# Turned blocks of e moved two units at a time, and the residual in four transfers, in a threshold attention and MLP mixer kernel

## The chip, the cores and the metric

The kernel runs as one program on one core of one Trainium2 chip. The metric is the device time of one execution in microseconds (us). Before the change three executions took 1266.56, 1267.58 and 1271.94 us; their median is 1267.58 us. Less is better.

A core has five engines that work side by side, each through an instruction list of its own, in order: TensorE (PE in the profile, with its weight loads as PEld), VectorE (DVE), ScalarE (ACT), GpSimd (POOL) and SyncE (SP). In this kernel SP computes nothing: it issues the DMA transfers, one after the other. "SPq" in the profile is SP's list.

## What is computed

For 8 batches b, 8 heads of 576 tokens and 64 columns, and then a mixer over 576 tokens x 512 columns, all in float32:

```python
scores = q @ k.T / 8
thresh = max(scores) - tau                      # per row
e      = exp(where(scores >= thresh, scores, -1e9) - max)
x      = (e / (sum(e) + 1e-9)) @ v              # heads side by side: 576 x 512
u      = x + (relu(x.T @ w_tok1) @ w_tok2).T    # token mixing, 576 -> 256 -> 576
out    = u + relu(u @ w_ch1) @ w_ch2            # channel mixing, 512 -> 1536 -> 512
```

## The kernel before, in words

**Units, rounds, groups.** A pair is two heads of a batch, so a batch has four pairs. The 2 x 576 score rows of two neighbouring pairs are cut into nine units of 128 rows; each unit has the scores of two heads, 128 x 1152 numbers. Two units with consecutive numbers make a round (`make_round`). Three units make a group (GU = 3), which is the size of one product with v (`values`, L365 and L370). Since nine is odd and groups have three units, the two units of a round lie in one group in six rounds of nine, and in two groups in the other three.

**One round.** PE forms the scores (L825). DVE takes the row maxima (mx, L842), POOL makes the bias (L848), ACT masks (L858) and takes exponentials with row sums (L868), DVE inverts the sums (rr, L276 and L277), and POOL scales e (L285). For batch 0, PE turns e (L300). For the seven later batches DVE turns each unit in 32 x 32 blocks into a tile T (`turn_blocks`, L315), and four transfers issued by SP put the blocks in their places in eT (`move`, L327). When a group's three units have landed, PE multiplies eT with v, and ACT or DVE drains the result into xT (L374).

**The mixer of the batch before** runs between the rounds: token mixing (L454, L472, with x turned by L395 and L401 and moved by L406 and L412), then for one block of 256 tokens channel mixing, `make_groups`: twelve products with w_ch1 (L948), drained through relu by ACT (L953) or DVE (L956), then eight with w_ch2 (L964), drained by DVE (L978) with the residual u added. The residual is turned by two DVE transposes into the tile `us` (L933) and moved to `ut` by eight transfers (L940). The sums are written over `us`, from which two stores go to the output (L988). `us` is one buffer, so the next batch's L933 waits for this batch's stores to land. The rest of the blocks is written aside (L531) and done at the end by `Late`, from about 905 us on; that part's instructions are not touched.

**What sets the order.** A planner, `Scheduler`, runs while the program is built. Each step is an `Op` with an engine, a cost in us, what it depends on and a rank. The planner keeps a clock for each engine, takes the step that can start first (then the one of lower rank), and writes the instructions of each engine in that order. For a DMA step, `dmas=(count, KB, issue)` says how many transfers it issues, how large each is, and what one costs SP; `transfer` lets eight be in flight and moves 214 KB per us. So a cost that is edited moves the order of everything planned after it. On the chip each engine then follows its list, and waits where an input is not there.

**Weights** come in as 31 pieces of 64-bit words through three raw buffers (`load_piece`, L200), and are converted by ACT, DVE and POOL (last at 174.75 us in the trace, POOL L239).

Of the kernel before, what the change touches and what calls it, by code (L numbers as in the profile page):

```python
# [17 lines left out]
P = 128  # L18
# [3 lines left out]
def kernel(  # L22
# [166 lines left out]
    def load_piece(i):  # L189
        if i >= len(pieces):  # L190
            return
        dst, src = pieces[i]
        rows = dst.shape[0]
        n = 1
        for d in dst.shape[1:]:
            n *= d
        if i == len(pieces) - 2:
            raw_at[i % NRAW] = att.tile([P, 2 * WMAX], U32, tag="spare", bufs=1, name="spare_a")
        raw = raw_at[i % NRAW][0:rows, 0 : n * (2 if wide(i) else 1)].bitcast(src.dtype)
        nc.sync.dma_start(out=like(raw, dst), in_=src)  # L200
        if wide(i):
            words = raw.bitcast(U32).rearrange("p (n w) -> p n w", w=2)
            h2 = high[0:rows, WMAX * (i % 2) : WMAX * (i % 2) + n]
            raws[i] = like(words[:, :, 0], dst), like(words[:, :, 1], dst), like(h2, dst)
        else:
            raws[i] = like(raw, dst)
# [103 lines left out]
    def turn_blocks(u):  # L310

        b, p0, t = units[u]
        e = st.pop(u)
        T = Ts[u] = att.tile([P, 4, NK * 32], F32, tag="T", bufs=3, name=f"T_{u}")
        nc.vector.transpose(  # L315
            out=T.rearrange("p a (c x) -> p c a x", c=NK), in_=e.rearrange("p (c a x) -> p c a x", c=NK, a=4)
        )

    def move(u):
        b, p0, t = units[u]  # L320
        key, place = (b, p0, t // GU), t % GU
        if place == 0:
            turned_e[key] = att.tile([P, GU, 4, NK * 32], F32, tag="eT", name=f"eT_{u}")
            eTs[key] = turned_e[key].rearrange("p n i (c x) -> p (n i) c x", c=NK)
        T = Ts.pop(u)
        for i in range(4):
            nc.sync.dma_start(  # L327
                out=turned_e[key][:, place, i, :], in_=T[32 * i : 32 * i + 32]
            )
# [389 lines left out]
    CONV = len(pieces)  # L719
    CR = (1, 1, 2)  # L720
# [26 lines left out]
    def make_conversion():  # L747
        for part in range(2):
            put_ac(0, part)
        for i in range(CONV):  # L750
            put_dv(i, 0)
            for part in range(1, 3):
                put_ac(i + 1, part - 1)
                put_dv(i, part)
            put(("pool", i), sched.op("pool", 1.27, lambda i=i: on_gpsimd(i), (key_op("dv", i, 2), key_op("ac", i, 0)), CR[0]))
            put_load(i + NRAW, (key_op("pool", i),))
# [18 lines left out]
    def make_pair(n):  # L775
# [32 lines left out]
        put(("split", n), sched.op("dve" if n >= NP else "pool", 0.25 if n >= NP else 0.5, lambda: split_middle(n), (key_op("loadv", n), free), 2))  # L808
# [110 lines left out]
    def make_groups(b, halves):  # L919
        uT = xTs[b]  # L920
        reads = []
        for i in range(NOW[b]):
# [3 lines left out]
            def new_us(s=s, i=i):  # L926
                s["us"] = work.tile([P, nt, 4, NCC * 32], F32, tag="us", bufs=1, name=f"us_{b}_{i}")

            def turn_u(s=s, i=i):
                new_us(s)  # L930
                s["ut"] = work.tile([P, nt, 4, NCC * 32], F32, tag="ut", bufs=1, name=f"ut_{b}_{i}")
                for m in range(nt):
                    nc.vector.transpose(  # L933
                        out=s["us"][:, m].rearrange("q a (c d) -> q c a d", c=NCC),
                        in_=uT[:, :, GR * i + P * m : GR * i + P * m + P].rearrange("q c (r a) -> q c a r", a=4),
                    )

            def move_u(k, s=s):
                for m in range(nt):
                    nc.sync.dma_start(  # L940
                        out=s["ut"][:, m, k, :], in_=s["us"][32 * k : 32 * k + 32, m]
                    )
# [30 lines left out]
            def leave(bank, t, c, s=s):  # L973
                if not b and "us" not in s:
                    new_us(s)
                o = s["us"][:, t].rearrange("q a x -> q (a x)")[:, P * c : P * c + P]
# [9 lines left out]
            def store(t, s=s, i=i):  # L986
                t0 = GR * i + P * t
                nc.sync.dma_start(out=out[b, t0 : t0 + P, :], in_=s["us"][:, t].rearrange("q a x -> q (a x)"))  # L988
# [3 lines left out]
            if b:  # L992
                turn = sched.op("dve", 1.2, turn_u, have + state["stores"] + state["adds"] + (converted if b == 1 else []), 5)
                reads.append(turn)
                moved = [sched.op("sp", 1.2, lambda k=k, m=move_u: m(k), (turn,), 1, dmas=(nt, 53, 0.645)) for k in range(4)]
# [17 lines left out]
            for t in range(nt):  # L1013
# [19 lines left out]
                stores.append(sched.op("sp", 0.35, lambda t=t, f=store: f(t), outs, 2, dmas=(1, 150, 0.35)))  # L1033
# [55 lines left out]
    def make_round(it):  # L1089
# [28 lines left out]
        for u in us:  # L1118
# [4 lines left out]
            if not b:  # L1123
# [15 lines left out]
                if t % GU == GU - 1:  # L1139
# [4 lines left out]
            deps += [key_op("T", u - 1), key_op("M", u - 3)]  # L1144
            put(("T", u), sched.op("dve", 1.31, lambda u=u: turn_blocks(u), deps, 4))
            put(
                ("M", u),
                sched.op(
                    "sp",
                    2.4,  # L1150
                    lambda u=u: move(u),
                    (key_op("T", u), key_op("V", G - 2) if t % GU == 0 else None),
                    0,
                    after=(key_op("M", u - 1),),
                    dmas=(4, 147, 0.645),
                ),
            )
            if t % GU == GU - 1:
# [329 lines left out]
```

## Time and profile before

| What | Value |
|---|---|
| three executions, median | 1267.58 us (1266.56 to 1271.94) |
| the profiled execution | 1273.39 us, of which the span from first to last instruction 1271.4 us |
| PE busy in the span | 1237.8 us |
| mean granted TensorE clock | 0.991 |
| eT<-T (L327): transfers, KB each, time to landing | 504, 144 KB, median 3.0 us (2.7 to 5.4) |
| ... SP's time for one issue | 542 / 602 / 2039 ns (least, median, most) |
| ut<-us (L940): transfers issued | 48, SP's median 602 ns, landing median 2.1 us |
| out_dram<-us (L988): transfers, landing | 16, median 3.2 us (2.0 to 4.6) |
| DVE T<-e (L315) | 126 times, median 1369 ns |
| DVE us<-xT (L933) | 12 times from 117 to 860 us, mean 1088 ns |

The page gives busy time per engine, the span in 40 slices, and the chain of work that ended last. A row of the timeline has start, duration, engine, line, operation and tile; what stands in brackets at its end is how long the engine was idle before it and what ended that. A row of the windows view has, for a stretch of time, each engine's busy us with the number of instructions, then the granted clock of TensorE (1.00 is full speed), the mean busy share of the DMA engines and GB/s.

### The profile page before, as it was taken

How to read it: one execution, taken by the hardware profiler on the slowest of the kernel's cores; microseconds unless marked ns; L12 is line 12 of the kernel's file. 1: busy time of each engine (PE TensorE's matmuls, PEld its weight loads, DVE VectorE, ACT ScalarE, POOL GpSimd, SP SyncE). 2: the span in 40 equal slices, each digit the busy share in tenths (PEclk: the TensorE clock that was granted, in tenths of full speed). 3: DMA queues.
4: the chain of work that ended last, by engine and by line, in shares of the span. 5: the costliest groups of instructions: out<-in, count | busy, mean ns of one | idle time of the engine just before them, and what ended most of it. 6: DMA issues, size and time to landing. Idle time of an engine off the chain costs nothing.

```text
span 1271.4 us, 21773 instructions
## 1 busy us (share of the span) xinstructions
PE 1237.8 (97%) x8150; PEld 1015.3 (80%) x8150; DVE 755.0 (59%) x1163; ACT 564.0 (44%) x1233; POOL 315.4 (25%) x518
## 2 busy tenths in 40 slices
PE   8888999999999999999989999999999999999998
PEld 7656778797678778878867777888988888888887
DVE  6699982656666667756666756761443534444443
ACT  6998862554645545556465455531110202011120
POOL 4565641232223333323323322410001010000100
PEclk9899999999999999999999999999999999999999
DMA  9546985366777786786776875750212101021011
GB/s 167 139 124 166 214 212 131 87 128 160 168 164 175 160 169 150 165 178 137 179 148 135 187 159 111 179 150 1 60 23 67 34 25 42 18 67 25 26 34 33
DMA packets 324216, 149.23 MB, mean 117 GB/s; under 512 B 223696, under 2 KB 316880, under 8 KB 324112
## 3 DMA queue, kind: packets, MB, share of 16 engines
q1 hardware_dynamic: 322240, 147.64, 50.5%
q8 instruction: 64, 1.05, 0.4%
q10 hardware_dynamic: 1872, 0.21, 0.1%
q14 instruction: 40, 0.33, 0.1%
HBM read 47.32 MB, written 13.50 MB: 48 GB/s over the span
## 4 chain that ended last, share of the span: by engine, by line
PE 78%; SPq 6%; DVE 5%; DMA 5%; ACT 4%; issue 2%; POOL 0%; DVEq 0%; ACTq 0%; POOLq 0%
PE bank L964 11%; PE bank L948 10%; PE o L1309 10%; PE sc L825 9%; PE bank L370 7%; PE hx L1309 6%; PE bank L454 5%; PE hmm L1309 4%; PE oz L1309 4%; PE hz L1309 4%; PE bank L472 4%; SPq L327 3%; PE bank L365 2%; DVE mx L842 2%; ACT e L858 2%
## 5 line engine op out<-in xcount | busy, mean ns | idle before, releaser
L285 POOL TENSOR_SCALAR e<-e,rr 128x576 f32<-128x576 f32 x288 | 213.2, 758 | 299.1 <-DVE rr L277 286.6
L858 ACT ACTIVATE e<-sc,bias 128x576 f32<-128x576 f32 x288 | 194.1, 740 | 156.8 <-POOL bias L848 155.1
L842 DVE TENSOR_REDUCE mx<-sc 128x2 f32<-128x1152 f32 x144 | 188.1, 1347 | 58.9 <-PE sc L825 58.4
L868 ACT ACTIVATE e<-e,ntau 128x576 f32<-128x576 f32 x288 | 220.4, 778 | 0.3
L315 DVE STREAM_TRANSPOSE T<-e 128x1152 f32<-128x1152 f32 x126 | 170.0, 1362 | 36.1 <-POOL e L285 22.2
L948 PE MATMUL bank<-xT,wc 128*128 128x256 f32 x768 | 181.0, 389 | 6.1 <-ACT g L953 5.1
L964 PEld LDWEIGHTS bank<-wc,g 128*128 128x128 f32 x1536 | 178.0, 192 | 10.4 <-issue 2.4
L964 PE MATMUL bank<-wc,g 128*128 128x128 f32 x1536 | 181.4, 276 | 0.9 <-DVE xT L483 0.4
L948 PEld LDWEIGHTS bank<-xT,wc 128*128 128x128 f32 x768 | 144.2, 192 | 36.6 <-ACT g L953 6.5
L825 PE MATMUL sc<-kT,qT 64*128 64x192 f32 (+1 forms) x1920 | 168.8, 337 | 2.7 <-ACT e L858 2.7
L825 PEld LDWEIGHTS sc<-kT,qT 64*128 64x128 f32 (+1 forms) x1920 | 140.8, 179 | 32.1 <-issue 16.3
L370 PE MATMUL bank<-eT,lv 128*64 128x384 f32 (+1 forms) x1024 | 135.2, 406 | 0.0
L1392 POOL TENSOR_TENSOR us<-us,ut 128x256 f32<-128x256 f32 x27 | 22.4, 843 | 391.8 <-DVE us L1230 391.8
L370 PEld LDWEIGHTS bank<-eT,lv 128*64 128x64 f32 x1024 | 74.4, 137 | 49.7 <-issue 41.3
L848 POOL TENSOR_SCALAR bias<-mx,toff 128x2 f32<-128x2 f32 x144 | 38.8, 270 | 197.9 <-DVE mx L842 193.3
L454 PE MATMUL bank<-x_sb,w 128*128 128x256 f32 x320 | 72.8, 383 | 0.3 <-DVE eT L305 0.2
L472 PE MATMUL bank<-w,a 128*128 128x192 f32 (+1 forms) x256 | 72.8, 418 | 0.2 <-DVE xT L483 0.2
L454 PEld LDWEIGHTS bank<-x_sb,w 128*128 128x128 f32 x320 | 59.8, 190 | 11.3 <-issue 1.3
L953 ACT ACTIVATE g<-bank 128x256 f32<-128x256 f32 x66 | 25.3, 383 | 92.9 <-PE bank L948 92.7
L1357 ACT ACTIVATE ga<-hmm 128x256 f32<-128x256 f32 x30 | 11.5, 384 | 116.8 <-PE hmm L1309 116.8
L1230 DVE TENSOR_TENSOR temps<-hx,temps 128x256 f32<-128x256 f32 x60 | 25.1, 418 | 56.7 <-PE hx L1309 56.6
L868 ACT ACTIVATION_READ_ACCUMULATOR e<-e,ntau 128x1 f32 x288 | 58.4, 203 | 0.0
(133 smaller groups left out, 1519.6 us busy)
## 6 DMA issues: line engine op xcount, KB each, us to landing
eT<-T SPq DMA_DIRECT2D x504, 144.0 KB, 3.0
lk<-in_k_dram SPq DMA_DIRECT2D x126, 72.0 KB, 2.9
lq<-in_q_dram SPq DMA_DIRECT2D x124, 72.0 KB, 3.1
out_dram<-us SPq DMA_DIRECT2D x32, 256.0 KB, 2.1
ut<-us SPq DMA_DIRECT2D x128, 64.0 KB, 2.1
lv<-in_v_dram SPq DMA_DIRECT2D x112, 72.0 KB, 2.6
spare<-in_moe_w_ch_dram SPq DMA_DIRECT2D x8, 512.0 KB, 3.9
extra<-in_moe_w_ch_dram SPq DMA_DIRECT2D x8, 512.0 KB, 3.8
```

What stands on the lines that cost most here:

```text
L285: nc.gpsimd.tensor_scalar(out=eh, in0=eh, scalar1=rr[:, h : h + 1], scalar2=1.0, op0=ALU.mult, op1=ALU.mult)
L315: nc.vector.transpose(out=T.rearrange("p a (c x) -> p c a x", c=NK), in_=e.rearrange("p (c a x) -> p c a x", c=NK, a=4))
L370: nc.tensor.matmul(to[r], lhsT=lv[:, j, :], rhs=e[j], start=False, stop=(c == NI - 1), skip_group_check=True)
L454: nc.tensor.matmul(to, lhsT=w1[:, t, P * m : P * m + P], rhs=x(t), start=(t == 0), stop=(t == NT - 1), skip_group_check=len(products) > 1,)
L472: nc.tensor.matmul(bank[:, n * i : n * i + n], lhsT=hidden[b][:, m, P * c : P * c + P], rhs=w2[:, m, lo : lo + n], start=(m == 0), stop=(m ...
L825: nc.tensor.matmul(sc[h][rows, f, HT * k : HT * k + HT], lhsT=qT[r, cols], rhs=kT[r, HT * f : HT * f + HT], start=True, stop=True, skip_gr ...
L842: nc.vector.tensor_reduce(out=mx[:, h], in_=sc[h][:, :, 0 : 2 * HT].rearrange("p f (k x) -> p k f x", k=2), axis=AX.XY, op=ALU.max)
L858: nc.scalar.activation(out=eh, in_=part[h], func=AF.Prelu, bias=bias[:, h], scale=SCALE, alpha=STEEP)
L868: nc.scalar.activation(out=eh, in_=eh, func=AF.Exp, bias=ntau, accum_out=rs[:, h, 0:1])
L948: nc.tensor.matmul(bank[:, 0:n], lhsT=wc1[:, j, c, :], rhs=uT[:, c, GR * i : GR * i + n], start=(c == 0), stop=(c == NCC - 1))
L964: nc.tensor.matmul(to, lhsT=s["g"][:, j, P * t : P * t + P], rhs=wc2[:, j, P * c : P * c + P], start=(j == 0 and b > 0), stop=(j == NJ - 1 ...
L1309: nc.tensor.matmul(ps, lhsT=l, rhs=r, start=start and x == 0, stop=x == len(pairs) - 1, skip_group_check=not start)
```

## The change

1. T holds two units, and there are two such buffers instead of three single ones. Where both units of a round lie in one group, one set of four transfers (128 x 2 x 288 numbers each) moves both, after the second has been turned; otherwise two sets of four, as before.
2. The residual goes in four transfers of twice the size instead of eight. For this `us` is laid out with the four column blocks outside and the two token tiles inside, so the stores read it in runs of 512 bytes instead of 2048.
3. The extra raw buffer `spare_a` is gone: the last two weight pieces use the other two buffers, one place on, and wait for the piece before in these.
4. Costs told to the planner: turning the residual 2.05 instead of 1.2, one unit 1.30 instead of 1.31, `split` 0.28 instead of 0.25, an issue 0.67 instead of 0.645, a store 270 KB and 0.55 instead of 150 KB and 0.35.

```diff
-        if i == len(pieces) - 2:
-            raw_at[i % NRAW] = att.tile([P, 2 * WMAX], U32, tag="spare", bufs=1, name="spare_a")
-        raw = raw_at[i % NRAW][0:rows, ...]
+        raw = raw_at[(i + (i >= len(pieces) - 2)) % NRAW][0:rows, ...]
...
-        T = Ts[u] = att.tile([P, 4, NK * 32], F32, tag="T", bufs=3, name=f"T_{u}")
+        if u % 2 == 0 or u - 1 not in Ts:
+            Ts[u - u % 2] = att.tile([P, 4, 2, NK * 32], F32, tag="T", bufs=2, name=f"T_{u}")
         nc.vector.transpose(
-            out=T.rearrange("p a (c x) -> p c a x", c=NK), in_=e.rearrange("p (c a x) -> p c a x", c=NK, a=4)
+            out=Ts[u - u % 2][:, :, u % 2, :].rearrange("p a (c x) -> p c a x", c=NK),
+            in_=e.rearrange("p (c a x) -> p c a x", c=NK, a=4),
         )
...
-    def move(u):
+    def move(us):
...
         for i in range(4):
-            nc.sync.dma_start(
-                out=turned_e[key][:, place, i, :], in_=T[32 * i : 32 * i + 32]
-            )
+            if len(us) == 2:
+                out, rows = turned_e[key][:, place : place + 2, i, :], T[32 * i : 32 * i + 32]
+            else:
+                out, rows = turned_e[key][:, place, i, :], T[32 * i : 32 * i + 32, :, us[0] % 2, :]
+            nc.sync.dma_start(out=out, in_=rows)
...
-            put_load(i + NRAW, (key_op("pool", i),))
+            if i + NRAW < CONV - 2:
+                put_load(i + NRAW, (key_op("pool", i),))
+            elif i + NRAW - 1 >= CONV - 2:
+                put_load(i + NRAW - 1, (key_op("pool", i),))
...
-                s["us"] = work.tile([P, nt, 4, NCC * 32], F32, tag="us", bufs=1, name=f"us_{b}_{i}")
+                s["us"] = work.tile([P, 4, nt, NCC * 32], F32, tag="us", bufs=1, name=f"us_{b}_{i}")
...
             def move_u(k, s=s):
-                for m in range(nt):
-                    nc.sync.dma_start(
-                        out=s["ut"][:, m, k, :], in_=s["us"][32 * k : 32 * k + 32, m]
-                    )
+                nc.sync.dma_start(out=s["ut"][:, :, k, :], in_=s["us"][32 * k : 32 * k + 32])
...
-                nc.sync.dma_start(out=out[b, t0 : t0 + P, :], in_=s["us"][:, t].rearrange("q a x -> q (a x)"))
+                nc.sync.dma_start(out=out[b, t0 : t0 + P, :].rearrange("q (c x) -> q c x", c=NCC), in_=s["us"][:, :, t, :])
...
-                turn = sched.op("dve", 1.2, turn_u, ...)
+                turn = sched.op("dve", 2.05, turn_u, ...)
-                moved = [sched.op("sp", 1.2, ..., (turn,), 1, dmas=(nt, 53, 0.645)) for k in range(4)]
+                moved = [sched.op("sp", 1.2, ..., (turn,), 1, dmas=(1, 107, 0.67)) for k in range(4)]
...
-                stores.append(sched.op("sp", 0.35, ..., outs, 2, dmas=(1, 150, 0.35)))
+                stores.append(sched.op("sp", 0.35, ..., outs, 2, dmas=(1, 270, 0.55)))
...
-            deps += [key_op("T", u - 1), key_op("M", u - 3)]
+            v = u - u % 2
+            deps += [key_op("T", u - 1), key_op("M", v - 4), key_op("M", v - 3)]
...
+        same = units[us[0]][0:2] == units[us[1]][0:2] and units[us[0]][2] // GU == units[us[1]][2] // GU
+        for moved in [us] if same else [us[0:1], us[1:2]]:
+            x = sched.op("sp", 2.4, lambda moved=moved: move(moved),
+                [key_op("T", u) for u in moved] + [key_op("V", G - 2) if t % GU == 0 else None],
+                0, after=(key_op("M", moved[0] - 1),), dmas=(4, 147 * len(moved), 0.67))
```

## The prediction

> **What bounds the kernel now.** First the page, for which engine is full.
>
> ```profile
> PE 1237.8 (97%) x8150; PEld 1015.3 (80%) x8150; DVE 755.0 (59%) x1163; ACT 564.0 (44%) x1233; POOL 315.4 (25%) x518
> PEclk9899999999999999999999999999999999999999
> ```
>
> PE is busy for 97% of the span, and the change does not touch PE's work: the written orders of the two kernels have 4272 PE instructions each, of the same kinds. So the change can only fill, or open, holes in PE's list, and the span of 1271.4 us has 33.6 us of them. Second, where the holes are, by the windows view. T is first written at 115.5 us and the last moves are issued at 840.6 us; before and after these nothing differs but the weights' last two pieces.
>
> ```profile
> 117.00:200.00 83.00, 82.24 (x622) 64.83 (x620) 69.81 (x103) 58.37 (x126) 41.01 (x54) 1.00 0.88 211
> 200.00:300.00 100.00, 98.48 (x732) 82.39 (x729) 51.22 (x70) 48.79 (x112) 24.02 (x42) 1.00 0.49 108
> 300.00:400.00 100.00, 95.95 (x723) 74.85 (x722) 68.49 (x96) 57.57 (x126) 30.87 (x54) 1.00 0.78 175
> 400.00:500.00 100.00, 99.03 (x746) 78.24 (x746) 66.08 (x99) 55.54 (x120) 30.70 (x54) 1.00 0.73 160
> 500.00:600.00 100.00, 99.38 (x745) 79.12 (x742) 65.47 (x93) 54.62 (x121) 30.30 (x52) 1.00 0.72 162
> 600.00:700.00 100.00, 96.75 (x700) 76.61 (x699) 67.48 (x97) 55.42 (x120) 27.89 (x51) 0.98 0.70 155
> 700.00:800.00 100.00, 97.44 (x708) 75.37 (x707) 66.01 (x93) 53.53 (x117) 28.65 (x51) 0.98 0.69 155
> ```
>
> The second number is PE's busy time. These seven rows lose 0.8, 1.5, 4.1, 1.0, 0.6, 3.3 and 2.6 us; 800 to 905 loses another 0.4 (104.62 of 105), 14.1 in all. Two rows also show a clock of 0.98, and finer windows say where: 0.59 from 641 to 645 and 0.58 from 746 to 750. In each, eight matmuls of L948 take 3.55 and 3.54 us, where 24 take 5.38 elsewhere in the chain (1.79 for eight): 1.76 us lost each time, 3.5 together. **All that this change can win is thus 17.6 us**, 1.4%.
>
> Third, what opens the holes: the timeline around the longest one, SP's rows and then the others'.
>
> ```profile
> 613.90 5.60 SPq L327 DMA_DIRECT2D eT<-T  x8
> 619.55 2.09 SPq L406 DMA_DIRECT2D x_sb<-extra  x2
> 621.75 0.66 SPq L531 DMA_DIRECT2D spill<-xT  x1
> 622.50 6.47 SPq L327 DMA_DIRECT2D eT<-T  x8
> 629.08 2.48 SPq L412 DMA_DIRECT2D x_sb<-extra  x4
> 631.60 0.59 SPq L988 DMA_DIRECT2D out_dram<-us  x1
> ```
> ```profile
> 620.44 0.25 DVE L978 TENSOR_TENSOR us<-bank,ut 128x128 f32<-128x128 f32 x1
> 634.41 2.08 DVE L933 STREAM_TRANSPOSE us<-xT 128x512 f32<-128x512 f32 x2 [3.95 <-DMA out_dram<-us]
> 641.09 3.55 PE L948 MATMUL bank<-xT,wc 128*128 128x256 f32 x8 [2.60 <-ACT g L953]
> ```
>
> The store's data is ready at 620.7 (L978), but SP issues back to back and comes to the store at 631.6. It lands at 634.4; until then DVE stands before L933 for 3.95 us, with T and the maxima behind it; ACT's masks wait for the maxima, the relu that empties PE's bank stands behind the masks, and PE loses 2.60 us and then 1.76 to the slow clock. So SP, which the page does not list as busy at all, is the queue behind this hole. At 744 us the same chain costs 2.08 + 1.76. The chain of waits names SP for three more: 1.23 us at 204 (SP is at four x_sb transfers while the loads of q and k wait, DVE's L269 waits for them, and the drain of PE's bank stands behind it), 1.88 at 337.5 (the product with v waits for blocks that SP issues from 331.20 to 336.7, eight in a row) and 0.99 at 362.6 (SP at ut and eT; DVE waits for a T buffer, then the drain is late). Two waits for v at 443 and 545 (0.63 and 0.35) are loads behind the same queue. **Holes behind SP: 13.2 us of the 17.6.**
>
> **The change part by part.**
>
> *SP's issues.* eT<-T goes from 504 to 336: 126 units are 42 pairs that share a group (168 transfers) and 42 single units (168). The residual's go from 48 to 24. One issue follows the other by 0.645 us (602 ns and 43 between), so SP saves 168 x 0.645 + 24 x 0.645 = 124 us of the some 640 us that it spends between 117 and 853 us. Of itself that is worth nothing to PE; it counts where SP is late.
>
> *What each hole becomes*, by the written order of the changed kernel. At 638: before the store stand now a pair (102, 103) and two single sets instead of four, and the pair (100, 101) further ahead: eight issues fewer, 5.2 us, more than DVE's 3.95 us wait. That hole goes: 2.60 + 1.76 = 4.4 us. At 337: the set that PE waits for is four issues instead of eight, 2.6 us less against a hole of 1.88, and PE's list has 24 matmuls of L964 put in ahead of that product: 1.9 us. At 204: the loads of q and k for that pair (9) now begin ahead of the moves of units 28 and 29, where they stood behind those of unit 33: 1.2 us. At 362: the loads that stood between the sets are gone ahead, and T has four places instead of three: 1.0 us. Sum 8.5 us. At 744: the store stands now behind eight loads, but L933 stands behind two maxima and two T as well; I count nothing. The waits for v: nothing.
>
> *What is added.* (a) A pair's first unit waits for the second to be turned. In the trace two T follow each other by 1.6 us (327.25, 328.85) or, with the maxima between, 3.8 (334.93, 338.74). Against that the pair needs 4 x 0.645 = 2.6 us less of SP. A transfer of double the size is not in the trace; where transfers queue, landings of 144 KB follow each other by some 0.4 us (an estimate from the landing times around 622 us), and the spill of 640 KB lands in 4.2 us against 3.0 for 144, 0.35 us more per 144 KB. So the pair lands between 2.6 - 1.6 - 0.4 = 0.6 us sooner and 3.8 + 0.4 - 2.6 = 1.6 later than its second unit does now. PE works at other things meanwhile (L948, L964, the mixer's products); where that cover is gone it costs up to 1.6 us a time. (b) The stores in runs of 512 bytes: not in the trace. Below: no change. Above: loads of q and k, 72 KB in runs of 128 bytes, land in 2.9 to 3.1 us against 2.1 for ut, 64 KB in longer runs, so 1 us. It costs only where L933 waits, five times now, and PE pays for two of these: 0 to 2 us. I take 0.5, for most of the waits start from a late issue. (c) DVE's and POOL's work stays: what T's new stride costs is unknown. L315 takes 1.18 ns per column (1362 for 1152) and L933 2.1 (1088 for 512), so the far end would be 1.1 us on each of 126; but L933 reads in steps of four, which L315 does not, and L315 writes jumping between four places already. I take no change. (d) The last weight piece but one waits for one conversion more (ended at 161.4 instead of 155.1). Its successor was issued at 165.64 only, and the last conversion needs 174.75; PE's hole in that row is 0.8 us. Nothing, with up to 2 us if the first product that waits for it (L962, at 175.0) comes later. (e) The planner writes a new order from 117 us on, and it has holes of its own that no row shows. The stretches in which nothing went wrong lost 0.6 to 1.0 us each, so such orders are good to that; I take 0.5 us for the four holes' places.
>
> *Sum:* 8.5 - 0.5 - 0.5 = **7.5 us less**: 1273.4 to 1265.9 for an execution like the profiled one. That one stands 5.8 us above the median, which has perhaps fewer of these holes; I keep the difference and predict 1267.6 - 7.5 = **1260 us**.
>
> *The clock.* By the Trainium skill, page "TensorE: Matmul & The Clock Gate", Part 1, the clock halves after an idle window of about 3.4 us, and shorter gaps do not matter. Here it fell to 0.59 and 0.58 behind holes of 2.60 and 2.08 us, and stayed at 1.00 behind 1.88 and 1.23. If the page's length held and the dip at 641 came from elsewhere, 1.8 us of the 7.5 would not be won; I go by the rows.
>
> **The rivals.**
>
> *Most of it goes (10%).* All SP-born holes close: 13.2 us, to 1254.5. For it: SP has 124 us to spare. Against: 744 is open, and the order is new.
>
> *The holes are dealt anew (38%).* What closes here opens there, because PE, DVE and ACT follow lists whose planned times are a little off: 0 to 6 us less, 1265. For it: the executions before lie 5.4 us apart with one order, and 97% is little room. Against: the queue named behind most holes is the one that is relieved.
>
> *Slower (11%).* SP works in order, so a pair's set that waits for its second T holds up everything behind it: loads, stores, the residual. It decides from 2.6 us of standing per pair, what the pair saves; with the maxima between two T it is 3.8. If that made every 100 us from 200 to 800 like the loud ones (4.1, 3.3 + 1.8, 2.6 + 1.8: 4.5 us), the loss would be 6 x 4.5 + 1.2 = 28 us instead of 17.6: 1278. Against: the planner knows the second T, and puts loads ahead of such sets, as at 204 and 362.
>
> That the issues do not fall is no rival: the written order has 336.
>
> **How the numbers follow.** Forecast 41%, at 1260; most 10%, at 1254.5; anew 38%, around 1265; slower 11%, around 1278. A change under 0.5% (6.3 us, 1261.2 to 1273.9) is about what a measurement of this kernel cannot tell from none. Faster by more: forecast and "most", less the forecast's part above 1261.2 and with the lower end of "anew", 50%; same 39%; slower 11%. The range runs from 1253.5 ("most", and the bounds of a and b on the good side) to 1269 (anew, with c and d against it); slower lies outside.
>
> **What would show it.** SP: 336 issues of eT, 24 of ut. No wait of DVE L933 for the store near 630 us and no clock under 0.9 there; PE over 98% from 300 to 400 and from 600 to 700. It would be wrong if PE's holes in 117 to 905 still sum to 14 us with other releasers, if SP waits for T grow by tens of us with PE waiting for eT behind them, or if the stores land 1 us later and L933 waits longer.

## The result, and the profile after

The changed kernel takes 1297.07 us (median of six, 1294.31 to 1299.87); the kernel before, run beside it, 1266.53 (six, 1265.70 to 1271.94). The ratio is **1.0235, 95% interval 1.0214 to 1.0257: slower by some 30 us**, where 7.5 us less was forecast, and beyond the range. The profiled execution took 1297.33 us, its span 1295.4. From the page of the changed kernel:

```profile
PE 1241.0 (96%) x8150; PEld 1017.4 (79%) x8150; DVE 753.2 (58%) x1158; ACT 565.0 (44%) x1238; POOL 315.4 (24%) x518
PEclk9899989999989999999999999999999999999999
```

PE's work is the same 8150 instructions. Its busy time grew by 3.2 us and its idle time (span less busy) from 33.6 to 54.4, by 20.8: together the 24.0 us by which this span is longer. The windows view of the changed kernel, in the stretches that the prediction used (second number: PE's busy time; the number ahead of the DMA share: the granted clock):

```profile
117.00:200.00 83.00, 73.42 (x519) 56.00 (x514) 67.24 (x102) 54.68 (x116) 40.26 (x52) 0.96 0.83 196
200.00:300.00 100.00, 99.88 (x768) 85.75 (x767) 50.35 (x65) 53.54 (x123) 24.54 (x44) 1.00 0.48 101
300.00:400.00 100.00, 90.96 (x676) 71.09 (x674) 55.73 (x77) 47.58 (x107) 25.86 (x45) 0.97 0.76 160
400.00:500.00 100.00, 95.08 (x688) 73.66 (x686) 62.24 (x87) 52.03 (x114) 28.63 (x51) 0.98 0.74 157
500.00:600.00 100.00, 95.16 (x709) 74.64 (x705) 66.92 (x97) 56.23 (x123) 28.99 (x52) 0.98 0.73 153
600.00:700.00 100.00, 97.08 (x720) 77.15 (x721) 68.15 (x96) 54.64 (x118) 29.58 (x53) 1.00 0.77 161
700.00:800.00 100.00, 97.29 (x726) 77.25 (x723) 67.26 (x98) 52.16 (x115) 30.23 (x53) 0.98 0.78 164
800.00:905.00 105.00, 105.00 (x742) 85.60 (x741) 58.83 (x75) 42.68 (x93) 20.54 (x36) 1.00 0.49 113
```

PE now loses 9.6, 0.1, 9.0, 4.9, 4.8, 2.9, 2.7 and 0.0 us, 34.1 in all against 14.1. The hole at 204 is gone. The one at 638 has to be looked for later, since the changed kernel is some 20 us behind by then: the residual's turning that began at 634.41 (L933, now L939) begins at 659.57, and the next one, 739.69 before, at 770.25. From the timeline after:

```profile
659.57 2.10 DVE L939 STREAM_TRANSPOSE us<-xT 128x512 f32<-128x512 f32 x2 [3.16 <-DMA out_dram<-us]
770.25 2.10 DVE L939 STREAM_TRANSPOSE us<-xT 128x512 f32<-128x512 f32 x2 [5.36 <-DMA out_dram<-us]
776.75 0.87 PE L367 MATMUL bank<-eT,vl 128*64 128x384 f32 x4 [2.38 <-DVE g L959]
```

The first store is issued at 656.23, though its data are ready at 646.3, and DVE still waits 3.16 us for it (3.95 before). PE happens to lose only 0.33 us behind that wait, at full clock, where it lost 2.60 and then 1.76. The second wait has grown from 3.95 to 5.36 us, and PE's hole behind it is 2.38 us (2.08 before).

Most new holes stand in front of one instruction, the product with v. Its row among the groups of instructions (the last part: idle time of PE just before it, and what ended most of it), first before, then after:

```profile
L365 PE MATMUL bank<-eT,vl 128*64 128x384 f32 (+1 forms) x256 | 44.4, 425 | 4.2 <-DMA x_sb<-extra 1.9 <-DVE xT L483 1.0 <-DMA lv<-in_v_dram 1.0
```
```profile
L367 PE MATMUL bank<-eT,vl 128*64 128x384 f32 (+1 forms) x256 | 46.5, 442 | 28.4 <-DMA eT<-T 12.0
```

4.2 us became 28.4; that is more than the whole growth of PE's idle time, and everything else lost less than before. So what the product waits for comes late: the blocks in eT, or what stands on the way to v, or, at 776.75, the store. The transfers show how. The page's DMA issues (number, size, median us from issue to landing) before, then after:

```profile
eT<-T SPq DMA_DIRECT2D x504, 144.0 KB, 3.0
```
```profile
eT<-T SPq DMA_DIRECT2D x168, 288.0 KB, 5.4
eT<-T SPq DMA_DIRECT2D x168, 144.0 KB, 3.0
```

And SP's issues of them, by source line (least, median and longest issue in ns, then the first and last start), before and after:

```profile
L327 SPq DMA_DIRECT2D eT<-T x504: 542/602/2039, 117.0 to 840.6; - x168
```
```profile
L331 SPq DMA_DIRECT2D eT<-T x336: 542/622/2902, 122.1 to 867.0; - x168
```

A pair's transfer lands 5.4 us after its issue, a single one 3.0. And the issue itself takes longer, up to 2.9 us. In the timeline, SP's rows and then the others' around the hole at 569.5 us:

```profile
561.99 4.85 SPq L331 DMA_DIRECT2D eT<-T  x4
566.94 3.43 SPq L120 DMA_DIRECT2D lv<-in_v_dram  x4
570.48 4.92 SPq L331 DMA_DIRECT2D eT<-T  x4
```
```profile
572.23 0.36 DVE L343 TENSOR_TENSOR vl<-lv,whose 128x64 int32<-128x64 int32 x2 [5.75 <-DMA lv<-in_v_dram]
572.51 0.75 DVE L959 TENSOR_SCALAR g<-bank 128x256 f32<-128x256 f32 x2
572.98 1.55 PE L367 MATMUL bank<-eT,vl 128*64 128x384 f32 x4 [3.51 <-DVE g L959]
```

Four issues of a pair take 4.85 us (0.63, 0.63, 1.77 and 1.70, and 0.04 between), where eight of a single unit's size took 5.60 before (613.90). Over all 42 pairs the median is 4.92 us, against 5.18 for eight in a row before. The loads of v stand behind them, DVE stands 5.75 us before its step on v (`vl`, L343 now), the relu that empties PE's bank stands behind that, and PE idles for 3.51 us. From 573 to 577 the granted clock is then 0.59. Summed over all rows of the traces from 100 us to the end, **SP spends 656.6 us in 1065 issues before and 675.5 us in 873 issues after.** The issues are the 192 fewer that were forecast, but the time that they were to save was not saved: the 504 issues of eT took 315.6 us and the 336 take 312.9, and the issues that stand behind them became longer (v from 67.5 to 78.9 us for 104 issues, k from 57.8 to 66.9 for 100, x_sb from 35.5 to 45.1 for 56).

### The profile page after: what moved, and what is told of

It reads as the page before. It is cut to its first block, busy times and chain, and to the rows that moved or that the text cites. A ratio compares the mean times of both kernels' runs of the same rounds, so it can differ in the third digit from the quotient of the medians.

```text
span 1295.4 us, 21416 instructions
## 1 busy us (share of the span) xinstructions
PE 1241.0 (96%) x8150; PEld 1017.4 (79%) x8150; DVE 753.2 (58%) x1158; ACT 565.0 (44%) x1238; POOL 315.4 (24%) x518
## 4 chain that ended last, share of the span: by engine, by line
PE 66%; SPq 11%; DVE 8%; DMA 5%; ACT 3%; issue 2%; POOL 0%; DVEq 0%; ACTq 0%; POOLq 0%
PE o L1319 10%; PE bank L967 10%; PE sc L831 7%; PE hx L1319 6%; SPq L331 6%; PE bank L951 5%; PE bank L372 5%; PE bank L456 5%; PE hz L1319 4%; PE oz L1319 4%; PE hmm L1319 4%; PE bank L474 3%; DVE mx L848 2%; DVE T L314 2%; DMA eT<-T 2%
## 5 line engine op out<-in xcount | busy, mean ns | idle before, releaser
L848 DVE TENSOR_REDUCE mx<-sc 128x2 f32<-128x1152 f32 x144 | 187.9, 1346 | 54.4 <-PE sc L831 54.2
L314 DVE STREAM_TRANSPOSE T<-e 128x1152 f32<-128x1152 f32 x126 | 170.3, 1364 | 45.8 <-POOL e L283 25.6
L951 PE MATMUL bank<-xT,wc 128*128 128x256 f32 x768 | 176.5, 384 | 1.1 <-DVE g L959 0.9
L951 PEld LDWEIGHTS bank<-xT,wc 128*128 128x128 f32 x768 | 142.8, 190 | 28.4 <-issue 4.9
L372 PE MATMUL bank<-eT,lv 128*64 128x384 f32 (+1 forms) x1024 | 142.1, 421 | 0.0
L372 PEld LDWEIGHTS bank<-eT,lv 128*64 128x64 f32 x1024 | 77.5, 142 | 55.2 <-issue 46.8
L367 PE MATMUL bank<-eT,vl 128*64 128x384 f32 (+1 forms) x256 | 46.5, 442 | 28.4 <-DMA eT<-T 12.0
```

The source lines that it names most:

```text
L314: nc.vector.transpose(out=Ts[u - u % 2][:, :, u % 2, :].rearrange("p a (c x) -> p c a x", c=NK), in_=e.rearrange("p (c a x) -> p c a x", c ...
L372: nc.tensor.matmul(to[r], lhsT=lv[:, j, :], rhs=e[j], start=False, stop=(c == NI - 1), skip_group_check=True)
L848: nc.vector.tensor_reduce(out=mx[:, h], in_=sc[h][:, :, 0 : 2 * HT].rearrange("p f (k x) -> p k f x", k=2), axis=AX.XY, op=ALU.max)
L951: nc.tensor.matmul(bank[:, 0:n], lhsT=wc1[:, j, c, :], rhs=uT[:, c, GR * i : GR * i + n], start=(c == 0), stop=(c == NCC - 1))
```

## The experiments

Ratios are to the kernel before, run beside them on the same chip, with 95% intervals. The chips differ from row to row, and the kernel before had medians from 1266.53 to 1270.66 us beside these runs, so a difference of two times from different chips is good to some 4 us.

| Kernel | Median, us (runs) | Ratio |
|---|---|---|
| changed | 1297.07 (6) | 1.0235 [1.0214, 1.0257] |
| e1: part 2 alone | 1268.04 (10) | 0.9984 [0.9968, 0.9999] |
| e6: part 3 alone | 1277.27 (10) | 1.0056 [1.0037, 1.0075] |
| e2: changed, every unit moved singly | 1277.22 (10) | 1.0059 [1.0038, 1.0080] |
| e3: part 3 and pairs, in e6's order | 1300.50 (4) | 1.0249 [1.0226, 1.0271] |
| e5: changed, a pair's set as eight | 1287.77 (4) | 1.0149 [1.0121, 1.0177] |
| e4: changed, planner told 1.25 for a pair's issue | 1299.27 (4) | 1.0242 [1.0215, 1.0270] |
| e7: changed, pairs only early in a group | 1290.64 (6) | 1.0138 [1.0110, 1.0166] |
| e8: changed, pairs only late in a group | 1296.76 (4) | 1.0209 [1.0176, 1.0242] |
| e12: changed, v loaded through ACT | 1299.77 (4) | 1.0239 [1.0209, 1.0268] |
| e13: e2, v loaded through ACT | 1297.36 (4) | 1.0209 [1.0176, 1.0243] |
| e11: e6 with five buffers of v | 1284.48 (4) | 1.0109 [1.0083, 1.0134] |
| e15: before, two of the new costs | 1270.40 (10) | 1.0010 [0.9993, 1.0027] |
| e16: before, SCORES 2.22 | 1277.56 (5) | 1.0067 [1.0044, 1.0090] |
| e18: e2, SCORES 2.22 | 1275.19 (6) | 1.0044 [1.0020, 1.0069] |
| e19: changed, SCORES 2.22 | 1297.89 (4) | 1.0232 [1.0203, 1.0261] |

**Which part.** Four kernels take the change apart.

m1: the sets of transfers by themselves, out of 32 partitions into 128 as the kernel moves T, and straight from 128 into 128.

```python
to[:, u, i, :] <- one[u][32 * i : 32 * i + 32]                 # eight of 144 KB
to[:, :, i, :] <- two[32 * i : 32 * i + 32]                    # four of 288 KB
run[:, i]      <- two[32 * i : 32 * i + 32]                    # four, runs of 2304 bytes
flat[:, 2 * i : 2 * i + 2, :] <- wide[:, 2 * i : 2 * i + 2, :] # four, straight
```

> Leaves out the whole computation; it writes zeros and only moves blocks, each set of transfers alone on SP's queue, three times: eight of 144 KB as the kernel before issues them for two units; four of 288 KB as the changed one; four of 288 KB with the target too in one run per row (2304 bytes); eight of 144 KB and four of 288 KB straight from 128 partitions to the same 128. Theory 1 (the transfers' bytes set the pace, and SP stands in the issue until there is room): the four last as long as the eight from first issue to last landing, some 7 to 8 us, with the third and fourth issue at 1.5 to 1.9 us each instead of 0.6. Theory 2 (the size is harmless, the planned order is at fault): the four are issued in 2.6 us and land in 4.5 to 5.5 us, the eight in 7 to 8. The last three sets tell whether the pace comes from the run length or from reading 32 partitions.

The timeline of m1 (SP's rows of the first of its three passes):

```profile
8.11 5.21 SPq L31 DMA_DIRECT2D to<-one  x8
...
18.52 4.69 SPq L36 DMA_DIRECT2D to<-two  x4
...
29.39 4.68 SPq L41 DMA_DIRECT2D run<-two  x4
...
44.06 2.46 SPq L51 DMA_DIRECT2D flat<-wide  x4
```

Half as many issues take 4.7 us instead of 5.2, so SP is freed of 0.5 us per pair, not 2.6. The first two issues of the four take 0.62 to 0.67 us each, the third 1.0 to 1.5 and the fourth 1.7 to 1.8 (m1 and m2 together): the later ones are held. The straight set of the same four sizes takes 2.46, so the hold belongs to these slow transfers, and not to 288 KB as such. The eight have landed 7.25 to 7.75 us after the first issue; the four 7.8 to 8.05 where nothing was issued soon behind them, and 9.1 to 9.6 where other transfers followed. Longer runs in the target do not mend it (7.8, and 8.9 to 9.2 with others behind).

The windows view says what fills the queue. While the eight move (m2, 53 to 57 us), the DMA engines are busy for 0.89 of the time and move 213 GB/s; while the four move, 0.91 and 174 (63 to 67) or 0.90 and 210 (64 to 68); in the straight set (m1, 45 to 48) 0.95 and 361. So transfers that spread fill the DMA engines at about half the straight rate. With these nearly full either way, fewer issues cannot make the set much shorter; that this is also what holds the issues is likely, but not shown.

e1: part 2 alone, on the kernel before.

```diff
-                for m in range(nt):
-                    nc.sync.dma_start(out=s["ut"][:, m, k, :], in_=s["us"][32 * k : 32 * k + 32, m])
+                nc.sync.dma_start(out=s["ut"][:, :, k, :], in_=s["us"][32 * k : 32 * k + 32])
```

> The kernel before with the residual in four transfers, the stores in runs of 512 bytes and their planned costs alone (part 2). Theories 1 to 3: like before, within 5 us. Theory 4 (the stores in short runs land later and hold DVE at the residual's turning): slower by over 6 us, DVE L939 waiting more than the 17.4 us of before.

1268.04 us: the residual in four, with its new costs and the stores in short runs, costs nothing. Its interval lies just below 1 (0.1 to 4 us less), which is within what a new order alone makes (below), so no gain is shown; no other version did better.

e6: part 3 alone, on the kernel before.

```diff
-        if i == len(pieces) - 2:
-            raw_at[i % NRAW] = att.tile([P, 2 * WMAX], U32, tag="spare", bufs=1, name="spare_a")
-        raw = raw_at[i % NRAW][0:rows, ...]
+        raw = raw_at[(i + (i >= len(pieces) - 2)) % NRAW][0:rows, ...]
```

> The kernel before with the raw buffer spare_a gone alone (part 3 of the change). Theories 1 and 2: like before, 1262 to 1272 us. Theory 3 (the last weight pieces come later and SP stands before them, as at the 7.7 us hole at 176 us of the changed kernel): slower by 5 to 10 us, with a hole of PE between 160 and 185.

7 us slower. In the timeline of e6, the last weight piece on POOL and PE's row just before it:

```profile
177.89 0.98 PE L826 MATMUL sc<-kT,qT 64*128 64x192 f32 x2 [3.75 <-ACT e L859]
178.94 1.30 POOL L237 TENSOR_TENSOR wc<-wc,spare 128x512 int32<-128x512 int32 x1 [1.19 <-ACT e L859]
```

The last piece begins at 178.94 us instead of 174.75 and PE has a hole of 3.75 us. The windows view of e6 gives 77.72 busy of 83 from 117 to 200, a loss of 5.3 against 0.8. Whether the 7 us are this or a new order is taken up below.

e2: the changed kernel, every unit moved singly.

```diff
-        for moved in [us] if same else [us[0:1], us[1:2]]:
+        for moved in [us[0:1], us[1:2]]:
```

> The changed kernel with every unit moved by itself by four transfers of 144 KB as soon as it is turned; all else of the change stays (T in two buffers of two units, residual, stores, weights, costs). Theories 1 and 2 (the pairs are at fault): back to 1262 to 1275 us, the loss of 30 us gone by 20 at least. Theories 3 and 4: still 1285 to 1300.

1277.22 us: with all of the change but the pairs, 20 of the 30 us are gone. The pairs are two thirds of the loss (three quarters by the ratios).

**What in the pairs.** The candidates: the transfers' size; the wait of the first unit for the second; and a planner that is told 0.67 for an issue that takes more.

e3: the kernel of e6 and its written order, with T in two buffers of two units as in the change; where both units share a group, nothing is issued at the first one's place and the pair's four at the second's.

```diff
+        if same and u == first:
+            return
         for i in range(4):
+            if same:
+                out, rows = turned_e[key][:, place - 1 : place + 1, i, :], T[32 * i : 32 * i + 32]
```

> The kernel before with the weights of the change (1277 us by themselves) and the pairs of the change, but planned as before: the first unit of a pair issues nothing, and the four transfers for both stand where the second unit's four stood. Theory 1 (later start and landing are what costs): 1287 to 1300. Theory 2 (the new plan is what costs): 1274 to 1282, like the weights alone.

1300.50 against 1277.27 for e6: **the pairs cost 23 us with no change in the planner's order.** PE's idle time grew from 35.2 to 54.1 us, of which 7.9 stand before the product with v and 5.5 before the products with w_ch1; PE's busy time grew by another 6.3, as its clock fell six times after 117 us, where it fell once in e6. The row of the product with v, e6 and then e3:

```profile
L363 PE MATMUL bank<-eT,vl 128*64 128x384 f32 (+1 forms) x256 | 44.4, 425 | 5.3 <-DMA x_sb<-extra 3.0 <-DVE xT L481 0.9 <-DMA lv<-in_v_dram 0.7
```
```profile
L371 PE MATMUL bank<-eT,vl 128*64 128x384 f32 (+1 forms) x256 | 45.8, 436 | 13.2 <-DMA eT<-T 5.7 <-DMA lv<-in_v_dram 4.2 <-issue 1.4
```

e5: the changed kernel, each pair's set issued as eight of 144 KB at the same place in the same written order.

```diff
+            for n, u in enumerate(us):
+                nc.sync.dma_start(out=turned_e[key][:, place + n, i, :], in_=T[32 * i : 32 * i + 32, :, u % 2, :])
```

> The changed kernel with each pair's set issued at the same place as eight transfers of 144 KB instead of four of 288 KB: the written order of all else and the wait for the second unit stay. Theory 1 as first put (the bytes set the pace, the number of issues is worth nothing): within 8 us of the changed kernel, 1289 to 1305. If instead the large transfers are themselves slower (last landing 9.1 to 9.4 us after the first issue alone on the queue, against 7.3 to 7.7 for eight): faster by over 8 us, 1275 to 1288. Theory 2 (the planner's price is wrong): the plan is as wrong as before, 1295 to 1305.

1287.77: twice as many issues are 9.3 us faster than the changed kernel, and SP spends less time on them (650.6 us in 1041 issues, against 675.5 in 873). So the size itself costs some 9 us, and fewer issues win nothing that makes up for it. The 10 us that are left between e5 and e2 go with the wait for the second unit and the order that the planner writes for pairs; no run here parts these two. That e3 loses its 23 us without a new order speaks for the wait.

e4: the planner told the true price.

```diff
-                dmas=(4, 147 * len(moved), 0.67),
+                dmas=(4, 147 * len(moved), 0.645 if len(moved) == 1 else 1.25),
```

> The changed kernel with the planner told what the trace of the changed kernel shows: 1.25 us for an issue of 288 KB and 0.645 for one of 144 KB, instead of 0.67 for both. Theory 2: most of the 20 us between the changed kernel and its version with single units (1277) comes back, 1274 to 1283. Theory 1: the transfers still start later and land later, so at most half comes back, 1286 to 1300.

1299.27: no better, so the planner's price is not the cause.

m2: single transfers alone, two from the same and from different 32 partitions, eight in two orders.

> Leaves out the whole computation; it writes zeros and only moves blocks, each set alone on the queue, twice, in this order: one transfer of 144 KB out of 32 partitions; one of 288 KB out of 32; one of 144 KB and one of 288 KB straight from 128 partitions to 128; two of 144 KB out of the same 32 partitions; two out of two different 32; eight of 144 KB with the same 32 twice in a row; eight with the four 32s in turn, twice (as the kernel before); four of 288 KB. Theory A (the pace of what leaves 32 partitions is the limit, and transfers out of different partitions run side by side): 288 KB out of 32 lands 1.2 to 1.6 us after 144 KB does, straight 0.3 to 0.5; two out of the same 32 land 0.8 us or more later than two out of different ones; the eight with the same 32 in a row last as long as the four of 288 KB, 9 us, and the eight in turn 7.3 to 7.7. Theory B (a large transfer is slow by its size, in its descriptors): same and different partitions make no difference, and both eights last 7.3 to 7.7.

The DMA view of m2 (number, size, median landing; `to<-src` spreads 32 partitions over 128, `to<-wide` is straight):

```profile
to<-src SPq DMA_DIRECT2D x42, 144.0 KB, 2.8
to<-src SPq DMA_DIRECT2D x10, 288.0 KB, 4.8
to<-wide SPq DMA_DIRECT2D x2, 288.0 KB, 2.5
to<-wide SPq DMA_DIRECT2D x2, 144.0 KB, 2.0
```

Straight, 144 KB more cost 0.47 us (2.02 to 2.49); spread, 1.15 when alone on the queue (2.7 and 2.8 to 3.9), and 2.0 by these medians, in which queued ones count. My theory here was that one transfer's reads of the same 32 partitions get in each other's way. It fell: two transfers from the same 32 land 0.69 us apart, from different ones 0.72; eight by rows of partitions 7.6 and 7.75, in turn 7.25 and 7.3. Why transfers that spread move at about half the straight rate stays open.

e7 and e8: the changed kernel with pairs only at places 0 and 1 of a group (e7), or 1 and 2 (e8), 21 of the 42 each.

```diff
+        same = same and units[us[0]][2] % GU == 0      # e7; == 1 in e8
```

> The changed kernel with a pair set only where the pair is units 1 and 2 of its group of three (28 of the 42 pairs or fewer); pairs that end a group go as single units. Theory 'late group' (what costs is that the group's last block lands later and PE's product with v waits): 1277 to 1284, near the version with single units (1277). Theory 'every pair' (each set costs SP and the queue alike, wherever it stands): in proportion to the number of pairs, half of the 20 us, 1285 to 1290.

> The other half: a pair set only where the pair is units 2 and 3 of its group, so that it ends it. Theory 'late group': most of the loss stays, 1290 to 1300. Theory 'every pair': 1285 to 1290.

1290.64 and 1296.76, 13 and 20 us over e2. A late pair completes its group, and it costs more (by 6 us, no more than a new order can make), but an early one has a third unit still to come and costs too. The two halves cost 33 together, where all pairs cost 20, so the costs do not add up, and neither "every pair" nor "the late ones alone" describes them.

**By which way it reaches PE.** In the view of waits, DVE's wait for v (total, times, longest) grew, before and after:

```profile
DVE vl L341 <- DMA lv<-in_v_dram: 29.2, 12, 10.1
```
```profile
DVE vl L343 <- DMA lv<-in_v_dram: 41.0, 17, 7.8
...
PE bank L367 <- DMA eT<-T: 12.0, 4, 7.7
```

So two ways are open: PE waits for eT itself, or DVE stands for loads of v that SP issues behind a pair's set. Where pairs are set against singles (e2 and changed, e6 and e3, e18 and e19, all from 117 to 905 us), DVE's wait for v grew by 28.7, 12.9 and 31.4 us, and PE's own wait for eT by 7.5, 5.2 and 2.4. Both grew each time, that for v more; how much of it reaches PE these sums do not say.

e12 and e13: the loads of v issued by ACT, with pairs (e12) and with singles (e13).

```diff
-                nc.sync.dma_start(out=lv[a:P:4], ...)
+                nc.scalar.dma_start(out=lv[a:P:4], ...)
```

> The changed kernel with the loads of v (batches 1 to 7) issued by ACT instead of SP, four times 0.6 us each for a pair of heads, planned so. The theory that the pair sets hurt through what stands behind them on SP (v comes late, DVE's L343 stands for it, 41 us in 17 waits in the changed kernel against 12 in the version with single units, and the maxima and drains behind L343 are late): DVE's wait for v falls under 15 us and the time to 1278 to 1288. The theory that the blocks' own lateness costs (PE's product with v waits for eT): the wait for v falls too, but the time stays at 1290 or more.

> The control: single units, all else of the change, and v loaded by ACT. Both theories: near the version with single units, 1270 to 1282; what ACT's 56 extra microseconds of issuing cost shows here.

1299.77 and 1297.36. DVE's wait for v fell to 18.0 us in e12 without any gain, but e13 lost 20 us by the same edit, and there the wait for v grew from 12.3 to 44.3 us. So loading v through ACT, planned anew, costs something of its own and hides what the edit gave. Most of that cost has nothing to do with the pairs: the first T begins at 132.2 us in e13 and at 114.7 in e2, at 128.7 in e12 and 115.1 in the changed kernel. From the first T to the closing part (its first product, L1319 in the changed kernel) e2 takes 793.3 us and the changed kernel 812.5, e13 798.6 and e12 795.2. So by that stage the pairs cost 19.2 us with v through SP, and nothing (3.4 less) with v through ACT. That speaks for the way through v. It does not settle it: the weights' end falls differently in this stage, and counted from the 19th T on the pairs cost 12.0 and 5.3 us.

e11: e6 with five buffers of v instead of four, so that its loads may start earlier.

```diff
-    VL = 4
+    VL = 5
```

> The kernel before with the weights of the change (1277 by themselves) and five buffers for v instead of four in the space that the raw buffer gave back, so that v can be loaded earlier. If late v costs the kernel before as well (29 us of DVE's waits): 1265 to 1274. If not: 1274 to 1280.

1284.48, above what either view expected and slower than e6 by 7, which is within what a new order alone makes: no gain from earlier loads of v is shown.

**How much is mere order.** Every edit of a cost rewrites the planner's order. In e16, e18 and e19 it also wrote 55 more of the products without use that fill PE's early waits (`keep_warm`; 8205 PE instructions instead of 8150), and in e12 and e13 60 more, so that part of a nudge's effect may be these.

e15: the kernel before with the changed costs of one unit's turning and of `split`. e16, e18 and e19: the kernel before, e2 and the changed kernel with one cost moved by 1%.

```diff
-            put(("T", u), sched.op("dve", 1.31, lambda u=u: turn_blocks(u), deps, 4))
+            put(("T", u), sched.op("dve", 1.3, lambda u=u: turn_blocks(u), deps, 4))
```
```diff
-    SCORES, VALUES = 2.2, 3.45
+    SCORES, VALUES = 2.22, 3.45
```

> The kernel before with two of the change's planned costs alone: 1.30 instead of 1.31 for turning a unit, 0.28 instead of 0.25 for splitting v. Nothing that any engine does changes but its order. If the order alone is worth little: 1265 to 1273. If any new order costs (the order before is a lucky one): 1275 to 1290.

> The kernel before with the planned cost of a round's scores 2.22 instead of 2.20, another new order of the same work. As for the last: 1265 to 1273 if the order alone is worth little, 1275 to 1290 if the order before is a lucky one.

> The changed kernel with single units, and the same nudge of the scores' cost. If the 20 us between pairs and singles are the pairs': 1272 to 1285 again. If they are an accident of two orders: anywhere from 1270 to 1300.

> The changed kernel with the same nudge. If the 20 us are the pairs': 1290 to 1304 again, over 12 us above the nudged version with singles. If they are an accident of two orders: anywhere from 1270 to 1300, and as likely under it.

The kernel before goes from 1268.21 to 1270.40 (the interval of its ratio includes 1) and 1277.56 by such nudges, so a rewritten order, with these products, makes between nothing and 9 us here. Singles stay at 1275 to 1277 (e2, e6, e18), pairs at 1297 to 1301 (changed, e3, e4, e19). **The 20 to 23 us of the pairs (22 to 25 by the ratios) stand in each of the three matched comparisons (e3 against e6, changed against e2, e19 against e18); the 7 us of the weights are within what order alone makes.** Most kernels with part 3 do finish the weights later (last conversion ends at 180.2 in e6, 180.8 in e2, 184.9 after; 176.0 before), and those that load v through SP lose 4.9 to 9.6 us from 117 to 200 (e12 3.1, e13 5.7), where kernels with the old buffers lose 0.5 to 2.6. So its hole is real; what it is worth in the whole time is not settled.

## Why the prediction was wrong, point by point

- **"SP saves 168 x 0.645 + 24 x 0.645 = 124 us" is the step that failed.** It took 0.645 us as the fixed price of an issue. It is a price that holds while the queue takes the data: for a pair's set it was 0.63, 0.63, 1.73 and 1.79 us (medians of the 42), so a pair's set saved SP 0.3 us where 2.6 were counted. What the 192 issues saved, longer issues of v, k and x_sb took back, and SP's total went from 656.6 to 675.5 us: 19 us more, in place of 124 less. m1 shows the same price with no engine at work beside it (5.2 to 4.7). (The "some 640 us" that SP was said to spend between 117 and 853 us are 583.3 by the rows.) The profile before had a warning that the prediction passed over: issues of L327 lasted up to 2039 ns where 602 is the median.
- **The price of double size.** "Some 0.4 us" per 144 KB more, from how landings follow each other and from the spill of 640 KB; measured 1.15 alone and 2.4 in the kernel (5.4 against 3.0). The rows around 622 us said more: the set of eight landed from 617.26 to 622.72, 0.78 apart on the mean, and 0.4 is the least of these gaps. The spill is no near row for a transfer that spreads 32 partitions over 128: m2's straight transfers show the small price (0.47), the spread ones the large. By the Trainium skill, page "DMA: Bandwidth & Descriptors", section "Anatomy of one DMA — SWDGE (gpsimd) path", measured there for another issuing engine, a transfer takes a fixed 2.0 us or so and its bytes at 436 GB/s. An estimate from that is 0.34 us for 144 KB more; the straight ones (0.47) come near it, the spread ones (1.15) do not.
- **The pair "lands between 0.6 us sooner and 1.6 later".** Both errors enter here, and one measure has them both: from its first issue to its last landing a pair's set takes 8.9 us in the changed kernel (median of 42), where eight singles in a row took 8.0 before. So the set itself ends 0.9 us later, where the prediction had it 2.2 us sooner (2.6 - 0.4). With that the same sum gives 2.5 to 4.7 us later (1.6 or 3.8, plus 0.9), and the cover of L948 and L964 does not last: up to 7.72 us of hole in front of one product. From the chain of waits and the timeline of the changed kernel at 176 us:

```profile
174.75 5.19 SPq L331 DMA_DIRECT2D eT<-T  x4
```
```profile
177.90 5.64 DMA eT<-T
```
```profile
183.68 1.55 PE L367 MATMUL bank<-eT,vl 128*64 128x384 f32 x4 [7.72 <-DMA eT<-T]
```

The fourth issue begins at 177.90, held behind the third, its data land 5.64 us later, and only then can PE go on.

- **The holes.** The one at 204 went, as forecast (1.2 us). At 638 PE's loss shrank from 4.4 to 0.3 us, but not by the forecast way, and this part came right by luck: the eight issues fewer were to end DVE's wait for the store, and it is 3.16 us still, for the issues ahead of it take longer than 0.645 us each (the pair's four 4.88, four of x_sb 3.69, eight single ones 6.08). At the next turning, where the prediction counted nothing, the wait and PE's hole behind it grew. From 300 to 400, where 2.9 us were to be won, the loss grew from 4.1 to 9.0.
- **(b) and (c)** held: with the stores in runs of 512 bytes e1 is no slower, their median landing is 3.2 us as before, and DVE's wait for a store (L939) is 9.5 us in all against 17.4, mostly because the last one, 6.52 us before, is down to 0.23; T's new stride left it at 1364 ns against 1362.
- **(d)** "Nothing, up to 2 us" was too little: that stretch lost 5.3 us in e6. The step looked only at when the piece was issued before, not at how late it would come once it had to wait.
- **(e)** 0.5 us for a new order was too little: of two nudges one made nothing that can be told from none, the other 9 us. That the quiet stretches lost 0.6 to 1.0 us each said how good this order is, not how good the next one would be.
- **The clock** fell again behind holes: to 0.50 from 359 to 363 us behind 5.06 us, to 0.59 from 573 to 577 behind 3.51, to 0.57 from 460 to 464 behind 2.58, and to 0.58 from 777 to 781 behind 2.38. It stayed at 1.00 behind 2.16 (342.44), though 2.08 had lowered it before, so the length of a hole alone does not decide. The dips come with holes shorter than the idle window of about 3.4 us that the Trainium skill names, page "TensorE: Matmul & The Clock Gate", Part 1, as the rows before had shown.
- **The rival "slower"** (11%, 1278) had the place right: loads behind a pair's set. Its deciding point, SP standing for the second T, does not go with the time: from 117 to 905 us SP waits 49.1 us for T before, 24.0 and 62.2 in the singles e2 and e18 (1277 and 1275 us), and 59.3 and 54.0 in the pairs of the changed kernel and e19 (1297 and 1298). That the first unit's blocks start later costs all the same, as far as e5 is slower than e2. What every run with pairs shows is the hold of the issues and the late landings. A range that took SP's price of a pair's issue from 0.645 to twice that would have shown that perhaps no SP time is won.

What stays open: how the 20 us divide between PE's wait for eT and DVE's for v, why the late and the early pairs do not add up, how the 10 us of e5 over e2 divide between the wait and the order, and why spreading transfers move at about half the straight rate.

## What to carry to other kernels

Before you count saved DMA issues as saved queue time, see whether an issue's duration is a fixed price or a hold by the data in flight: look at its longest rows and at whether larger transfers of the same shape are issued as fast. Joining two transfers makes the first wait for the second's input and both land together and later; that is a loss wherever the consumer was nearly starved. In a kernel whose main engine is 97% busy under a planned order, nudge one cost by 1% first: what that moves is the least that an edit's effect must exceed.

## What the runs showed of the hardware that was not expected

- An issue on SP's queue takes longer while earlier, slowly draining transfers are in flight: of four spreading transfers of 288 KB the third takes 1.0 to 1.5 us to issue and the fourth 1.7 to 1.8, the first two 0.62 to 0.67; four straight ones of that size take 2.46 in all.
- A transfer from 32 partitions to 128 takes 2.7 to 2.8 us for 144 KB and 3.9 for 288 KB alone; from 128 to 128 it takes 2.02 and 2.49. With the DMA engines busy for 0.89 of the time and more, sets of the former move 174 to 213 GB/s in m2, and a set of the latter 361 in m1.
- Two such transfers from the same 32 partitions are no slower than from different ones (0.69 and 0.72 us apart).
